# Second block: where the cycle without one two-head maximum stands in a hand-written order of attention work

## The chip, the cores and the metric

The kernel runs on one core of one Trainium2 chip. The metric is the device time of one execution in microseconds, the median of three runs. A profile is one further execution with the hardware profiler; its span is the time from the first to the last instruction on the engines.

## The reference, cut to what matters

Two independent attention blocks on 2048 tokens of width 512, with 32 heads of 16 each. Block A lets a query see the 256 keys up to itself, block B lets it see all keys. The outputs stand side by side.

```python
def _B_ref(x, wqkv, wo):
    B, S, D = x.shape
    H = 32
    Dh = D // H
    qkv = (lambda x, *d: x.transpose(*d))((x @ wqkv).reshape(B, S, 3, H, Dh), 2, 0, 3, 1, 4)
    q, k, v = qkv[0], qkv[1], qkv[2]
    scores = jnp.einsum("bhqd,bhkd->bhqk", q, k) * (Dh ** -0.5)
    p = _softmax(scores, axis=-1)
    o = jnp.einsum("bhqk,bhkd->bhqd", p, v)
    return (lambda x, *d: x.transpose(*d))(o, 0, 2, 1, 3).reshape(B, S, D) @ wo
```

`_A_ref` is the same with a mask: where a key lies after the query or 256 or more before it, the score is set to -1e9. The result is `concatenate([a, b], axis=-1)`, all in float32.

## The kernel before, in words

**Units and steps.** Work is cut into units (g, c): four heads (g of 8) by 512 queries (c of 4), so block B has 32 units. A unit takes 16 steps, one for each tile of 128 keys, 512 steps in all for block B, and `ns` counts four scores to a step. In a step TensorE multiplies keys by queries for four heads (`scores`, L572, one bank of PSUM each), ScalarE takes the exponential of each bank (L579), and TensorE, a step or two later, weighs the values with them (`weigh2`, L603). An extra row of ones in the values gives the sum for the softmax.

**The maxima.** The softmax needs the maximum of each row of scores before the exponential. So every score is also computed one unit ahead of its use, with queries on the partitions (`max2`, matmul L406), and VectorE reduces it (L410) into a tile `mt`. An item of this pass is 4 heads by 128 queries by 512 keys; a unit has 16 items, and there are 496 items from the second unit on (`mx`). An item consists of two halves of two heads each, counted by `half`. There are two ways to do a half:

- `M`: two matmuls into banks 3 and 4 and one VectorE reduction over both. The next `M` has to wait until this reduction has read the two banks.
- `m`, twice: one matmul into bank 5 or 6 and one reduction of one head each.

When both halves of an item are there, GpSimd (POOL) folds it into the running maximum (`chunk_max`: L514 for the first key chunk of four, otherwise L517, L518, L519). After the sixteenth item of a unit GpSimd splits the result into three bfloat16 parts (`low_finish`: L526 to L529, tile `nm`).

**The rows.** The maximum enters the scores as three extra rows of the queries' operand `oq`. `max_rows` makes them: TensorE transposes `nm` (L539, one load of weights and one matmul), ScalarE copies the result (L541), and two DMAs on SyncE's queue write it into `oq` (L546). The unit's scores wait for these DMAs. In the order below this is the letter `T`, and it does something once in a unit.

**The order.** All engines take their instructions in program order, so the order written for TensorE decides what waits for what. For block B it is written out as strings, worked through letter by letter: `s` one score, `M` and `m` as above, `2` and `4` a half or a whole step of weighing, `T` the rows, `x` one matmul of an output projection of block A or B, twelve to a tile of 128 tokens (L217).

- `ORDER` is the plain cycle of two steps: 8 `s`, 2 `M`, 4 `m`, so four halves. Its halves come in this sequence: a pair of `m`, `M`, a pair of `m`, and after `T` and one more `s` the second `M`.
- `ORDER_B` is `ORDER` without that second `M`: three halves in two steps.
- `ORDER_F` is the fed cycle of eight steps with a tile of twelve `x`: 32 `s`, 10 `M`, 12 `m`, so sixteen halves. It begins with `m s M`. It is chosen when a step divisible by 8 begins and a tile is due.
- `LAST` and `LAST_F` have no maxima and are used when all 496 items are done.

A tile is due (`due`, L1096) when its planned time has come and its operands are ready by the planner's own clock, or when one is begun. The step's number also releases loads and normalisations (`plan`, `settle`), and normalising puts three GpSimd operations into its queue (L690, L692, L693 of `normalise_now`).

**Which cycles occur.** Block B begins with step 2 of its loop; eleven plain cycles cover steps 2 to 23, sixteen fed cycles steps 24 to 151, 170 plain cycles steps 152 to 491, and cycles without maxima the rest. `ORDER_B` stands in the code of before, under the condition that a tile is due at the third plain cycle out of four; at the cycle of step 22 that isn't so yet, and behind it the fed cycles follow each other directly. So before has no `ORDER_B` cycle at all.

```python
ORDER = "ssm4mssMs2msms2TsM"
ORDER_B = "ssm4mssMs2msms2Ts"
ORDER_F = "msMs2mssm2ssMms4ssMms4ssMms4ssMsm4ssMms4mssMsxxxxxxTxxMsmss4MssmsxxxxsMsms4s"
```

Of the kernel before, what the change touches and what calls it, by code (L numbers as in the profile page):

```python
# [20 lines left out]
HG = 4  # L21
# [15 lines left out]
STEP = 2.36  # L37
# [3 lines left out]
# [3 lines that stand above are left out]
# [105 lines left out]
def attention_kernel(ctx: ExitStack, tc: tile.TileContext, xT, wqk, wv, wo, out):  # L149
# [9 lines left out]
    M = Model()  # L159
    ready = {}  # L160
    obank = [None]
    ns = 0
# [232 lines left out]
    def max2(g, c, qt, kc, heads, ps):  # L395

        m = maxima(1, g, c).rearrange("p (a r) q k -> p a r q k", a=2)
        early = g == 0 and c == 0 and heads[0] < 2
        if not early:
            follow(("k", 1, g))  # L400
            follow(("q", 1, g, c))
        for n, j in enumerate(heads):
            r, a = divmod(j, 2)
            rows = slice(ROW[a], ROW[a] + KS)
            q, k = (qe[0], ke()) if early else (opq[1, g, c][:, r], opk2(g)[:, r])
            nc.tensor.matmul(ps[:, n], q[rows, 128 * qt:128 * qt + 128], k[rows, kc * QC:kc * QC + QC], start=True,  # L406
                             stop=True)
            t = M.pe("h", 118, 0 if early else loaded(1, g, c))
        r, a = divmod(heads[0], 2)
        nc.vector.tensor_reduce(out=m[:, a:a + len(heads), r, qt, kc], in_=ps, axis=AX.X, op=ALU.max)  # L410
        return M.run("DVE", 65 + 533 * len(heads), t)
# [150 lines left out]
    def scores(b, g, c, kt, j, heads=1, pieces=((),)):  # L562

        n = f"{b}_{g}_{c}_{kt}"
        pr, a0 = divmod(j, 2)
        banks = [M.take("e") for _ in range(heads)]
        ps = [view(bank) for bank in banks]
        w = QC if b else sum(x[3] for x in pieces)
        for k, col, q0, n1 in [(kt, 0, 0, QC)] if b else pieces:
            for x in range(heads):  # L570
                rows = slice(ROW[a0 + x], ROW[a0 + x] + (KM if (b, g, c) > (1, 0, 0) else KS + 2))
                nc.tensor.matmul(ps[x][:, col:col + n1], opk2(g)[rows, pr, 128 * k:128 * k + 128],  # L572
                                 opq[b, g, c][rows, pr, q0:q0 + n1], start=True, stop=True)
            t = M.pe("h", 235 if b else 12 + n1 / 2.4, ready["q", b, g, c])
        if a0 == 0:
            pts[b, g, c, kt, pr] = sb.tile([128, 2, QC], F32, name=f"p_{n}_{pr}", tag="p", bufs=2 * AHEAD)
        p = pts[b, g, c, kt, pr]
        for x in range(heads):
            nc.scalar.activation(p[:, a0 + x, :w], ps[x][:, :w], AF.Exp, scale=SCALE)  # L579
            done = M.run("ACT", 60 + w / 1.2, t)  # L580
            M.release(banks[x], done)
        if b == 0:

            for d, sign, base in ((0, 1, 0), (2, -1, -1)):
                cols = [col // 128 + x for k, col, q0, n1 in pieces for x in range(n1 // 128)
                        if 4 * c + q0 // 128 + x - k == d]
                for x in cols:
                    v = p[:, :, 128 * x:128 * x + 128]
                    nc.gpsimd.affine_select(out=v, in_=v, pattern=[[0, 2], [sign, 128]], compare_op=ALU.is_ge,  # L589
                                            fill=zero_fill, base=base, channel_multiplier=-sign)  # L590
                    done = M.run("Pool", 360, done)
        ready["p", b, g, c, kt] = done
# [137 lines left out]
    proj = []  # L730
# [23 lines left out]
    def settle():  # L754

        while soon and soon[0][0] <= M.t["PE"]:
            heapq.heappop(soon)[2]()
# [34 lines left out]
    def pop():  # L792
        now[0], _, f, a = heapq.heappop(todo)
        f(*a)
        made.add((f, *a))

    gen = [None, None]
# [19 lines left out]
    def operands(it):  # L817

        f, b, *a = it
        if f == project_qk:  # L820
            keys = [(("w", b, a[0], a[1]), ("x", b, a[2], i)) for i in range(4)]
            t = slots_st[0] - 2700 + LAND_V
        elif f == project_v:
            keys = [(("w", b, "v", i), ("x", b, a[0], i)) for i in range(4)]
            t = slots_v[0] - 2700 + LAND_V
        else:
            keys = [(("w", b, "o", i), ("o", b, i, a[0])) for i in range(4 if len(a[1]) == 1 else 3)]
            t = 0
        at = [max(ready.get(x, M.NEVER) for x in k) for k in keys]
        return M.NEVER if max(at) >= M.NEVER else max(t, *(x - FEED * i * (f != project_out) for i, x in enumerate(at)))  # L830
# [115 lines left out]
    nm = k = nb = ne = n1 = 0  # L946
# [141 lines left out]
    mx = [(NA + 1 + i // 16, *units[NA + 1 + i // 16][1:], *divmod(i % 16, NQC)) for i in range(16 * turn)]  # L1088
    ns, nq, nm, fed = n1, n1 - 8, AHEADM, 0
    half, odd, full = 2 * AHEADM, None, set()  # L1090
    t0 = M.t["PE"] - 1000 * ns // HG * STEP
    rows, order = [], ORDER
    for u, g, c, qt, kc in mx[:AHEADM]:
        chunk_max(g, c, qt, kc)

    def due():  # L1096
        return gen[0] or proj and proj[0][0] <= ns // HG * STEP and operands(proj[0][3]) <= M.t["PE"]

    while nq < 4 * len(steps):
        if nm == len(mx) and len(M.banks["e"]) == 3:  # L1100
            M.banks["e"] += [M.t["PE"] + 4000] * 2
        if nm == len(mx):
            order = LAST_F if due() and not rows else LAST
        else:
            f, g = order == ORDER_F, ns // HG % 8
            order = ORDER_F if due() and g == 0 and nm + 8 <= len(mx) else ORDER
            if order == ORDER and not f and g == 6 and due() and nm + 10 <= len(mx):
                order = ORDER_B
        for x in order:
            k = ns // HG  # L1110
            if x == "s" and k < len(steps):
                if ns % HG == 0:
                    t = k * STEP
                    M.t["PE"] = max(M.t["PE"], t0 + int(1000 * k * STEP))
                    settle()
                    while todo and todo[0][0] <= t:
                        pop()
                scores(1, *steps[k], ns % HG)
                ns += 1
            elif x in "Mm" and (half < 2 * len(mx) or x == "m" and odd is not None):  # L1120
                if x == "M":
                    y = half
                    half += 1
                    max2(*mx[y // 2][1:], (2 * (y % 2), 2 * (y % 2) + 1), ps_all[:, 3:5])
                elif odd is None:
                    y, odd = half, half
                    half += 1
                    max2(*mx[y // 2][1:], (2 * (y % 2),), room()[1][:, None])
                else:
                    y, odd = odd, None  # L1130
                    max2(*mx[y // 2][1:], (2 * (y % 2) + 1,), room()[1][:, None])
                if y != odd:
                    full.add(y)
                while {2 * nm, 2 * nm + 1} <= full:
                    u, g, c, qt, kc = mx[nm]
                    chunk_max(g, c, qt, kc)
                    nm += 1
                    if nm % 16 == 0:
                        low_finish(g, c)
                        rows.append((k + 1, (1, g, c)))  # L1140
            elif x == "T":
                if rows and rows[0][0] + (nm == len(mx)) <= k:
                    max_rows(*rows.pop(0)[1])
            elif x == "x" and (gen[0] or due()):
                now[0] = k * STEP
                advance()
                fed += 1
                if fed == 12:
                    fed = 0
                    advance()  # L1150
                    if nm < len(mx):
                        t0 += 2410
            elif x.isdigit():
                if 0 <= nq < 4 * len(steps):
                    g, c, kt = steps[nq // 4]
                    q = nq % 4
                    weigh2(g, c, kt, 128 * q, 128 * (q + int(x)))
                    if kt == NT - 1 and q + int(x) == 4:
                        unit_end(1, g, c)
                nq += int(x)  # L1160
# [29 lines left out]
```

## Time and profile before

| what | value |
|---|---|
| time, median of 3 runs | 1818.95 us (1818.33 to 1819.58) |
| the profiled execution's own time | 1819.65 us |
| span of the profiled execution | 1817.9 us |
| ScalarE busy in the span | 1420.0 us (78%) |
| GpSimd busy in the span | 688.8 us (38%) |
| VectorE: L410, the maxima of block B | 1203.4 us, 1482 reductions |
| TensorE: L572, L406, L603 | 739.4, 636.3, 586.8 us |

The rows of a view of instructions read: start and length in microseconds, engine, line, operation, tiles and shapes, count of merged instructions, and in brackets the idle time of the engine before it with what ended it. PE is TensorE's matmuls, PEld its loads of weights. A row that merges several instructions of an engine runs from the start of the first to the end of the last. A view of windows gives for each stretch its bounds, its length, then each engine's busy time with the number of instructions, the granted clock of TensorE and the DMA share. Reductions on VectorE are pipelined, so one starts up to 0.1 us before the end of the one before.

### The profile page before, as it was taken

The numbers are of one execution on the slowest core, as the hardware profiler recorded it, in microseconds if no ns is written. First come the engines' busy times: TensorE is split into PE (matmuls) and PEld (weight loads), VectorE is DVE, ScalarE is ACT, GpSimd is POOL, SyncE is SP. The second block draws the span as 40 slices with busy tenths as digits, with TensorE's granted clock in tenths as the row PEclk, the third lists the DMA queues.
The fourth block names the chain that finished last, engine by engine and source line by source line (L and its number), as shares of the span: only waits on it lengthen the run. The fifth ranks groups of instructions, "written<-read, shape, count | busy, mean of one in ns | idle before, by whom it ended". The sixth has DMA issues, their size and how long they took to land. (4 is left out here: it accounts for less than half of the span.)

```text
span 1817.9 us, 38163 instructions
## 1 busy us (share of the span) xinstructions
PE 1798.2 (99%) x13992; PEld 901.4 (50%) x13992; DVE 1515.2 (83%) x2189; ACT 1420.0 (78%) x2773; POOL 688.8 (38%) x2054
## 2 busy tenths in 40 slices
PE   7999999999999999999999999999999999999999
PEld 5766666666664444444444444444444444444446
DVE  4655676766689889999989999999999999999911
ACT  4367777565659788888889988998898998899883
POOL 0167787554655453223222423332222333222310
PEclk9999999999999999999999999999999999999999
DMA  7756767454553225111300311030030121000012
GB/s 239 198 177 200 225 206 220 152 164 140 180 182 104 71 74 117 45 42 40 75 28 26 74 47 39 29 78 17 16 76 29 35 63 37 17 24 15 30 34 97
DMA packets 128569, 166.47 MB, mean 92 GB/s; under 512 B 22946, under 2 KB 58258, under 8 KB 128370
## 3 DMA queue, kind: packets, MB, share of 16 engines
q1 hardware_dynamic: 128382, 164.04, 31.2%
q8 instruction: 110, 1.80, 0.4%
q14 instruction: 77, 0.63, 0.1%
HBM read 94.49 MB, written 68.19 MB: 89 GB/s over the span
## 5 line engine op out<-in xcount | busy, mean ns | idle before, releaser
L579 ACT ACTIVATE p<-ps_all 128x512 f32<-128x512 f32 x2432 | 1257.8, 598 | 163.1 <-PE ps_all L572 116.0
L410 DVE TENSOR_REDUCE mt<-ps_all 128x1 f32<-128x512 f32 (+1 forms) x1482 | 1203.4, 884 | 53.3 <-PE ps_all L406 38.2
L572 PE MATMUL ps_all<-oq,opk 51*128 51x512 f32 (+3 forms) x2752 | 739.4, 406 | 2.4 <-ACT p L579 2.1
L406 PE MATMUL ps_all<-opk,oq 48*128 48x512 f32 x2016 | 636.3, 433 | 1.0 <-DVE mt L410 1.0
L603 PE MATMUL ps_all<-p,vt 128*32 128x256 f32 (+1 forms) x5672 | 586.8, 487 | 0.0
L572 PEld LDWEIGHTS ps_all<-oq,opk 51*128 51x128 f32 (+1 forms) x2752 | 376.8, 185 | 227.7 <-ACT p L579 196.0
L406 PEld LDWEIGHTS ps_all<-opk,oq 48*128 48x128 f32 x2016 | 303.1, 185 | 277.7 <-issue 149.7
L517 POOL TENSOR_TENSOR md<-mt,mm 128x4 f32<-128x4 f32 x372 | 75.9, 204 | 612.2 <-DVE mt L410 611.2
L589 POOL TENSOR_SCALAR_AFFINE_SELECT p<-p 128x256 f32<-128x256 f32 x480 | 178.9, 406 | 221.9 <-ACT p L579 220.4
L603 PEld LDWEIGHTS ps_all<-p,vt 128*32 128x32 f32 x5672 | 112.7, 108 | 218.1 <-issue 208.1
L217 PE MATMUL ps_all<-x,w 128*128 128x512 f32 x768 | 195.1, 404 | 10.3 <-ACT w L170 10.2
L463 DVE COPY_PREDICATED ps_all<-mone,ps_all 128x256 f32<-128x256 uint16 x224 | 95.0, 424 | 85.8 <-PE ps_all L454 84.1
L217 PEld LDWEIGHTS ps_all<-x,w 128*128 128x128 f32 x768 | 141.2, 190 | 50.5 <-ACT w L170 10.2
L464 DVE TENSOR_REDUCE mt<-ps_all 128x2 f32<-128x512 f32 x224 | 155.2, 693 | 7.7
L279 ACT ACTIVATE raw<-ps_all 128x512 f32<-128x512 f32 x56 | 33.5, 598 | 108.8 <-PE ps_all L217 105.9
L217 PE MATMUL ps_all<-w_o,x_o 128*128 128x512 f32 x384 | 102.3, 407 | 0.2 <-ACT ob L715 0.2
L217 PE MATMUL ps_all<-w_v,x 128*128 128x512 f32 x384 | 96.4, 400 | 0.3 <-DVE w_v L171 0.3
L618 PE MATMUL ps_all<-p,vt 128*32 128x384 f32 (+2 forms) x1408 | 96.4, 390 | 0.0
L518 POOL TENSOR_SCALAR md<-md 128x4 f32<-128x4 f32 x372 | 81.7, 220 | 32.6
L454 PE MATMUL ps_all<-opk,oq 48*128 48x384 f32 (+2 forms) x512 | 88.1, 373 | 1.3 <-DVE mt L464 1.1
L519 POOL TENSOR_TENSOR mm<-mm,md 128x4 f32<-128x4 f32 x372 | 74.8, 201 | 31.0
L217 PEld LDWEIGHTS ps_all<-w_o,x_o 128*128 128x128 f32 x384 | 68.0, 188 | 26.9 <-issue 8.0
(63 smaller groups left out, 718.3 us busy)
## 6 DMA issues: line engine op xcount, KB each, us to landing
parts<-st SPq DMA_DIRECT2D x64, 512.0 KB
opk<-parts SPq DMA_DIRECT2D x128, 128.0 KB
oq<-parts SPq DMA_DIRECT2D x128, 128.0 KB
od<-ou SPq DMA_DIRECT2D x64, 256.0 KB
vd<-vst SPq DMA_DIRECT2D x32, 272.0 KB
opk<-parts SPq DMA_DIRECT2D x128, 64.0 KB
oq<-parts SPq DMA_DIRECT2D x128, 64.0 KB
t<-od SPq DMA_DIRECT2D x32, 256.0 KB
```

The source lines that it names most:

```text
L217: nc.tensor.matmul(ps, l(u), r(v), start=start and k == 0, stop=stop and k == n - 1)
L406: nc.tensor.matmul(ps[:, n], q[rows, 128 * qt:128 * qt + 128], k[rows, kc * QC:kc * QC + QC], start=True, stop=True)
L410: nc.vector.tensor_reduce(out=m[:, a:a + len(heads), r, qt, kc], in_=ps, axis=AX.X, op=ALU.max)
L454: nc.tensor.matmul(two[:, a, 0:w], opq[b, g, c][rows, r, 128 * qt:128 * qt + 128], opk2(g)[rows, r, t0:t1], start=True, stop=True)
L463: nc.vector.copy_predicated(two[:, :, 256:384], later, two[:, :, 0:128])
L464: nc.vector.tensor_reduce(out=m[:, :, r, qt, 0], in_=two[:, :, 128:384], axis=AX.X, op=ALU.max)
L518: nc.gpsimd.tensor_scalar(d, d, 0.0, None, op0=ALU.max)
L572: nc.tensor.matmul(ps[x][:, col:col + n1], opk2(g)[rows, pr, 128 * k:128 * k + 128], opq[b, g, c][rows, pr, q0:q0 + n1], start=True, stop= ...
L579: nc.scalar.activation(p[:, a0 + x, :w], ps[x][:, :w], AF.Exp, scale=SCALE)
L589: nc.gpsimd.affine_select(out=v, in_=v, pattern=[[0, 2], [sign, 128]], compare_op=ALU.is_ge, fill=zero_fill, base=base, channel_multiplier ...
L603: nc.tensor.matmul(o[32 * j:32 * j + 32, q0:q1], vt[(g // 2) % 2][:, kt, vc:vc + 32], pts[1, g, c, kt, j // 2][:, j % 2, q0:q1], start=kt ...
L618: nc.tensor.matmul(o[32 * j:32 * j + 32, q0:q0 + w], vt[(g // 2) % 2][:, kt, vc:vc + 32], pts[b, g, c, m, j // 2][:, j % 2, col:col + w], ...
```

## The change

`due` can look ahead by a number of steps, with a twentieth more: a tile counts as due if its planned time and its operands' time lie no more than 2.1 steps (4.96 us of the planner's clock) ahead. The cycle of a step with remainder 6 by 8 becomes `ORDER_B` the first time that a tile is due two steps ahead, and never again (`shorter`). The conditions on a preceding fed cycle and on ten items left are dropped.

```diff
@@ -1089,12 +1089,13 @@
     ns, nq, nm, fed = n1, n1 - 8, AHEADM, 0
     half, odd, full = 2 * AHEADM, None, set()
     t0 = M.t["PE"] - 1000 * ns // HG * STEP
-    rows, order = [], ORDER
+    rows, shorter = [], True
     for u, g, c, qt, kc in mx[:AHEADM]:
         chunk_max(g, c, qt, kc)
 
-    def due():
-        return gen[0] or proj and proj[0][0] <= ns // HG * STEP and operands(proj[0][3]) <= M.t["PE"]
+    def due(ahead=0):
+        d = (ahead + ahead / 20) * STEP
+        return gen[0] or proj and proj[0][0] <= ns // HG * STEP + d and operands(proj[0][3]) <= M.t["PE"] + 1000 * d
 
     while nq < 4 * len(steps):
         if nm == len(mx) and len(M.banks["e"]) == 3:
@@ -1102,10 +1103,10 @@
         if nm == len(mx):
             order = LAST_F if due() and not rows else LAST
         else:
-            f, g = order == ORDER_F, ns // HG % 8
+            g = ns // HG % 8
             order = ORDER_F if due() and g == 0 and nm + 8 <= len(mx) else ORDER
-            if order == ORDER and not f and g == 6 and due() and nm + 10 <= len(mx):
-                order = ORDER_B
+            if shorter and g == 6 and due(2):
+                order, shorter = ORDER_B, False
         for x in order:
             k = ns // HG
             if x == "s" and k < len(steps):
```

**At the entry of the first fed cycle.** TensorE's rows around step 24, where the plain cycle of step 22 ends and the first fed cycle begins; L406 is a matmul of the maxima, L572 a score, L603 weighing. Before:

```order
L572 MATMUL ps_all<-oq_0_1_5847,opk_74 128x512
L406 MATMUL ps_all<-opk_74,oq_0_2_6059 128x512 x3
L572 MATMUL ps_all<-oq_0_1_5847,opk_74 128x512
L406 MATMUL ps_all<-opk_74,oq_0_2_6059 128x512 x2
L572 MATMUL ps_all<-oq_0_1_5847,opk_74 128x512
L603 MATMUL ps_all<-p_0_1_6_0_7034,vt_76 32x256 x2
```

The same rows of TensorE at the same place after the change:

```order
L572 MATMUL ps_all<-oq_0_1_5847,opk_74 128x512
L406 MATMUL ps_all<-opk_74,oq_0_2_6059 128x512
L572 MATMUL ps_all<-oq_0_1_5847,opk_74 128x512
L406 MATMUL ps_all<-opk_74,oq_0_2_6059 128x512 x2
L572 MATMUL ps_all<-oq_0_1_5847,opk_74 128x512
L603 MATMUL ps_all<-p_0_1_6_0_7034,vt_76 32x256 x2
```

Of the three maxima matmuls in the second row, two are the plain cycle's second `M`; they are gone, and the fed cycle's first `m` is left. The two matmuls of the fourth row are the fed cycle's first `M`.

**From there on.** The number of halves to be done is the same, so every place in the order now holds the half that stood one place later before, until the maxima end. Sixteen halves fill a fed cycle and four a plain one, so nothing evens this out. TensorE's rows in the plain cycle that holds the `T` of unit (7, 0), long after the fed cycles; `oq_7_0` names the unit whose maxima are being taken, `oq_7_1` the next one, `oq_6_3` the unit whose scores run. Before:

```order
L406 MATMUL ps_all<-opk_75,oq_7_0_18189 128x512 x2
L572 MATMUL ps_all<-oq_6_3_17739,opk_74 128x512 x2
L406 MATMUL ps_all<-opk_75,oq_7_1_18631 128x512
L603 MATMUL ps_all<-p_6_3_10_0_19014,vt_77 32x512 x2
L603 MATMUL ps_all<-p_6_3_10_1_19027,vt_77 32x512 x2
L406 MATMUL ps_all<-opk_75,oq_7_1_18631 128x512
...
L539 LDWEIGHTS nm_7_0_19067
L539 MATMUL ps_all<-ident,nm_7_0_19067 48x128
```

And TensorE's rows at the same place after the change:

```order
L406 MATMUL ps_all<-opk_75,oq_7_0_18176 128x512 x2
L572 MATMUL ps_all<-oq_6_3_17726,opk_74 128x512 x2
L406 MATMUL ps_all<-opk_75,oq_7_0_18176 128x512
L603 MATMUL ps_all<-p_6_3_10_0_19007,vt_77 32x512 x2
L603 MATMUL ps_all<-p_6_3_10_1_19024,vt_77 32x512 x2
L406 MATMUL ps_all<-opk_75,oq_7_0_18176 128x512
...
L539 LDWEIGHTS nm_7_0_19082
L539 MATMUL ps_all<-ident,nm_7_0_19082 48x128
```

The last half of unit (7, 0) was the second `M` of the cycle before; it is now the first pair of `m` of the cycle that holds the transposition, which itself has not moved.

At the end of the maxima one half is left over: steps 492 and 493 form a plain cycle with two `m` in place of two `LAST` cycles, the last `T` moves from the end of step 493 to the end of step 494, and the `LAST_F` cycles begin at step 495 in place of 494.

**On GpSimd.** A normalisation's three operations (L690, L692, L693) stay where the step's number puts them in GpSimd's queue, while the last item of a unit moves back past them. GpSimd's rows around the end of the maxima of unit (1, 0), in a fed cycle; `md_0_3_2` and `md_0_3_3` are the fifteenth and the sixteenth item, `t_3_3` is block A's normalisation of the last chunk, and L526 begins the splitting. Before:

```order
L517 TENSOR_TENSOR md_0_3_2_8138<-mt_1_0_7689,mm_0_7711 128x4
L518 TENSOR_SCALAR md_0_3_2_8138<-md_0_3_2_8138 128x4
L519 TENSOR_TENSOR mm_0_7711<-mm_0_7711,md_0_3_2_8138 128x4
L517 TENSOR_TENSOR md_0_3_3_8157<-mt_1_0_7689,mm_0_7711 128x4
L518 TENSOR_SCALAR md_0_3_3_8157<-md_0_3_3_8157 128x4
L519 TENSOR_TENSOR mm_0_7711<-mm_0_7711,md_0_3_3_8157 128x4
L526 CAST nm_1_0_8161<-mm_0_7711 128x2x8
L527 TENSOR_TENSOR nr_1_0_8162<-mm_0_7711,nm_1_0_8161 128x16
L528 CAST nm_1_0_8161<-nr_1_0_8162 128x2x8
L529 TENSOR_TENSOR nm_1_0_8161<-nr_1_0_8162,nm_1_0_8161 128x2x8
L690 TENSOR_TENSOR t_3_3_8110<-t_3_3_8110,bl_3_3_8112 128x512
L692 CAST x_o_3_3_8182<-t_3_3_8110 128x512
```

GpSimd's rows at the same place after the change:

```order
L517 TENSOR_TENSOR md_0_3_2_8135<-mt_1_0_7692,mm_0_7752 128x4
L518 TENSOR_SCALAR md_0_3_2_8135<-md_0_3_2_8135 128x4
L519 TENSOR_TENSOR mm_0_7752<-mm_0_7752,md_0_3_2_8135 128x4
L690 TENSOR_TENSOR t_3_3_8103<-t_3_3_8103,bl_3_3_8105 128x512
L692 CAST x_o_3_3_8168<-t_3_3_8103 128x512
L693 TENSOR_TENSOR x_o_3_3_8168<-t_3_3_8103,x_o_3_3_8168 128x512
L517 TENSOR_TENSOR md_0_3_3_8182<-mt_1_0_7692,mm_0_7752 128x4
L518 TENSOR_SCALAR md_0_3_3_8182<-md_0_3_3_8182 128x4
L519 TENSOR_TENSOR mm_0_7752<-mm_0_7752,md_0_3_3_8182 128x4
L526 CAST nm_1_0_8186<-mm_0_7752 128x2x8
L527 TENSOR_TENSOR nr_1_0_8187<-mm_0_7752,nm_1_0_8186 128x16
L528 CAST nm_1_0_8186<-nr_1_0_8187 128x2x8
```

The normalisation of `t_3_3` stood behind the splitting and now stands between the fifteenth and the sixteenth item.

## The prediction

> **What bounds the kernel now.** I read the page first, then windows, then single rows. The page gives the span and TensorE's share:
>
> ```profile
> span 1817.9 us, 38163 instructions
> PE 1798.2 (99%) x13992; PEld 901.4 (50%) x13992; DVE 1515.2 (83%) x2189; ACT 1420.0 (78%) x2773; POOL 688.8 (38%) x2054
> ```
>
> A PE that is 99% busy is no proof of a bound, since matmuls overlap. So I cut block B into stretches: fed cycles of eight steps, the whole plain stretch, and the steps behind the maxima. Each row gives the length, then the busy time of each engine, and the granted clock ahead of the DMA share.
>
> ```profile
> core 0: us, PE busy (x) PEld busy (x) DVE busy (x) ACT busy (x) POOL busy (x), PEclk, DMA share, GB/s
> 592.81:618.67 25.86, 24.86 (x151) 9.80 (x150) 20.40 (x24) 17.46 (x34) 12.64 (x32) 0.87 0.12 36
> 618.67:639.66 20.99, 20.99 (x150) 9.18 (x148) 19.13 (x23) 17.61 (x34) 10.93 (x25) 1.00 0.32 102
> 639.66:661.63 21.97, 21.49 (x151) 9.18 (x150) 19.12 (x23) 17.43 (x35) 13.71 (x36) 1.00 0.33 79
> 661.63:682.65 21.02, 21.02 (x150) 9.11 (x149) 19.16 (x23) 17.61 (x34) 10.91 (x25) 1.00 0.23 77
> 682.65:704.06 21.41, 21.41 (x151) 9.18 (x150) 19.13 (x23) 17.43 (x34) 12.22 (x34) 1.00 0.32 81
> 595.90:602.72 6.82, 6.82 (x36) 2.25 (x36) 3.95 (x6) 3.87 (x8) 4.60 (x11) 0.50 0.10 35
> 937.00:1731.00 794.00, 794.00 (x6819) 333.78 (x6819) 792.93 (x1028) 715.22 (x1402) 230.69 (x966) 1.00 0.15 38
> ```
>
> Two things stand out. In the plain stretch VectorE is busy 792.93 of 794.00 us: it is the bound there, with 1.07 us to spare. In fed cycles it is not (19.13 of 20.99 us); TensorE is, with twelve more matmuls. And the first fed cycle takes 25.86 us where the third and the fifth, which like the first hold a transposition, take 21.97 and 21.41: something is lost at its entry, the place that the change is about.
>
> **The entry, which gets faster.** TensorE's and VectorE's rows there:
>
> ```profile
> 592.03 0.94 PE L406 MATMUL ps_all<-opk,oq 48*128 48x512 f32 x3
> 592.81 0.40 PE L572 MATMUL ps_all<-oq,opk 51*128 51x512 f32 x1
> 594.21 0.50 PE L406 MATMUL ps_all<-opk,oq 48*128 48x512 f32 x2 [1.00 <-DVE mt L410]
> 592.34 1.81 DVE L410 TENSOR_REDUCE mt<-ps_all 128x1 f32<-128x512 f32 x2
> ```
>
> The x3 holds the plain cycle's last `M`; VectorE reduces it last in the row that ends at 594.15. The fed cycle's own `M` needs the same two banks, and TensorE stands still for 1.00 us. Soon after, the window from 595.90 shows a granted clock of 0.50 for 6.82 us, which costs about half of that, 3.41 us. Together 4.41 us, and the windows say 25.86 - 21.41 = 4.45: the two agree. With the change the `M` in front is gone, its banks were read a half cycle earlier, and the wait has no cause. What is late next is VectorE, still one one-head reduction behind at the entry; against that the cycle in front has one reduction less. I take **-4.5 us**, with ends of -3 (a shorter wait stays) and -5.5 (the cycle in front is shorter by all its reduction). The reduction is not saved, only done later.
>
> The Trainium skill, "TensorE: Matmul & The Clock Gate", section "HAM oscillation", gives as its rule that no idle gap of TensorE over about 3.4 us should occur. Here 1.00 us of idle time stands ahead of the half clock, so the trace does not agree. By that rule the clock would not hang on this wait, and the term would be about -1.0 us.
>
> **The transpositions, which get slower.** The rest of the program runs one half later. In the plain stretch the cycle that holds `T` is this:
>
> ```profile
> 1621.07 1.27 DVE L410 TENSOR_REDUCE mt<-ps_all 128x1 f32<-128x512 f32 x2
> 1623.99 1.85 DVE L410 TENSOR_REDUCE mt<-ps_all 128x1 f32<-128x512 f32 x2
> 1621.29 0.21 POOL L517 TENSOR_TENSOR md<-mt,mm 128x4 f32<-128x4 f32 x1 [1.53 <-DVE mt L410]
> 1622.99 0.22 POOL L529 TENSOR_TENSOR nm<-nr,nm 128x16 bf16<-128x16 f32 x1
> 1623.67 0.10 PEld L539 LDWEIGHTS <-nm 128*48 128x48 bf16 x1 [0.41 <-POOL nm L529]
> 1624.18 0.40 PE L406 MATMUL ps_all<-opk,oq 48*128 48x512 f32 x1
> ```
>
> Before, the unit's last half is an `M` that ends as the pair of the first row begins. GpSimd folds and splits from 1621.29 to 1623.21, and TensorE comes to L539 at 1623.67, 0.46 us later: covered. After, the last half is the pair of the first row. Its end is 1622.34, two one-head reductions later. Their spacing is 1.27 us less the length of one:
>
> ```profile
> L410 DVE TENSOR_REDUCE mt<-ps_all x1018: 622/680/1227, 936.9 to 1729.9; 128x2 f32<-128x1024 f32 x169, 128x1 f32<-128x512 f32 x1
> ```
>
> So 1.27 - 0.68 = 0.59 us each and 1.19 for two. GpSimd's chain then ends at 1623.21 + 1.19 = 1624.40, L539 starts at 1624.45 (0.05 after it, as at 654.58 below), and TensorE waits 0.78 us longer. Behind the waiting L539 stand a score and the second `M`. In before that `M` is ready at 1624.18 + 0.40 = 1624.58, and VectorE is through with the pair of the second row at about 1624.6: nothing is in stock. So VectorE idles as long as TensorE does, and since it is the bound of this stretch the loss stays. ScalarE waits for the score too, but has 794.00 - 715.22 us of slack. The rows' copy and two DMAs move with L539, and so do the scores that need them. With 0.03 us taken off I count 0.75 us for each. How many there are:
>
> ```profile
> L539 PE MATMUL ps_all<-ident,nm x21: 236/237/237, 950.7 to 1698.5; 128*48 128x128 bf16 x21
> L539 PE MATMUL ps_all<-ident,nm x7: 236/237/237, 654.6 to 909.2; 128*48 128x128 bf16 x7
> ```
>
> In the plain stretch 21, so **+15.8 us**; ends are 0 (if VectorE makes it up) and 21 x 0.78 = 16.4. Seven, with one more in the first fed cycle, lie in fed cycles. One of them:
>
> ```profile
> 735.32 0.20 POOL L517 TENSOR_TENSOR md<-mt,mm 128x4 f32<-128x4 f32 x1 [0.51 <-DVE mt L410]
> 737.01 0.22 POOL L529 TENSOR_TENSOR nm<-nr,nm 128x16 bf16<-128x16 f32 x1
> 737.77 0.23 POOL L514 TENSOR_SCALAR mm<-mt 128x4 f32<-128x4 f32 x1 [0.54 <-DVE mt L410]
> 739.44 0.24 PE L539 MATMUL ps_all<-ident,nm 128*48 128x128 bf16 x1
> ```
>
> L514 belongs to the next half's item, so 737.77 is when the last fold can begin after the change. From 735.32 to 737.23 the chain takes 1.91 us, so it ends at 739.68, and L539 starts at 739.73: 0.29 us late. That such a wait is paid in full shows in the unit whose GpSimd is late already:
>
> ```profile
> 654.31 0.22 POOL L529 TENSOR_TENSOR nm<-nr,nm 128x16 bf16<-128x16 f32 x1
> 654.58 0.24 PE L539 MATMUL ps_all<-ident,nm 128*48 128x128 bf16 x1 [0.48 <-POOL nm L529]
> ```
>
> Its fed cycle took 21.97 us against 21.41: 0.56 us for 0.48 of idle matmul time. There the chain is held up by something else and I add nothing. Six units at 0.3 make **+1.8 us**, with ends 0 and 2.4.
>
> The eighth is unit (1, 0), where a normalisation now stands ahead of the last item:
>
> ```profile
> 691.00 1.29 POOL L693 TENSOR_TENSOR x_o<-t,x_o 128x512 fp32r<-128x512 f32 x1
> 692.24 0.23 POOL L517 TENSOR_TENSOR md<-mt,mm 128x4 f32<-128x4 f32 x1
> 693.13 0.20 POOL L517 TENSOR_TENSOR md<-mt,mm 128x4 f32<-128x4 f32 x1
> 688.96 1.28 POOL L690 TENSOR_TENSOR t<-t,bl 128x512 f32<-128x512 f32 x1 [0.35 <-DMA bl<-rl]
> 697.02 0.24 PE L539 MATMUL ps_all<-ident,nm 128*48 128x128 bf16 x1
> ```
>
> Three such operations take 692.29 - 688.96 = 3.33 us, one item 0.89. After the item at 692.24 come 3.33 us and the 1.91 of the chain: 693.13 + 3.33 + 1.91 + 0.05 = 698.42, so L539 is **1.4 us** late; 0 if the operations are done sooner, 3.3 if their DMA lands late.
>
> **The end.** Behind the maxima the last `T` comes one step later:
>
> ```profile
> 1734.39 0.73 PE L572 MATMUL ps_all<-oq,opk 51*128 51x512 f32 x3
> 1736.99 0.24 PE L539 MATMUL ps_all<-ident,nm 128*48 128x128 bf16 x1
> 1740.80 0.73 PE L572 MATMUL ps_all<-oq,opk 51*128 51x512 f32 x4
> ```
>
> A `LAST` step takes 1736.99 - 1734.39 = 2.6 us. After the change two steps run as a plain cycle, at the stretch's pace of (1698.5 - 950.7) / 20 / 16 = 2.34 a step, and one remains. From T to the unit's first score there are then 3.81 us in place of two steps more, for the copy and two DMAs. I count **0**, with ends of -1 and +1.
>
> **The sum.** -4.5 + 15.8 + 1.8 + 1.4 + 0 = +14.5 us on the profiled execution's 1819.65 us, whose span of 1817.9 is 1.75 shorter. That is 1834.1. The median of the runs is 0.7 us lower, so I predict **1833.4 us**.
>
> **The rivals.** *The waits at `T` are absorbed.* GpSimd's chain may be released earlier than I take it, or TensorE may come to `T` later, once VectorE is behind it. Then only the entry's gain is left: 1819.0 - 4.5 = 1814.5. It speaks for it that 0.46 us of cover exist, against it that the reductions' order and the distance to `T` can be read off; it decides where the delay falls below 0.46 us, and it is 1.19. I give it 0.11. *Half of it is absorbed*, for instance because TensorE's faster stretches refill VectorE: +8 - 4.5 + 1.6, so 1824; 0.10. Near zero, 1816 to 1822, lies 0.06.
>
> *The new waits bring down the clock.* TensorE would be idle about as long before `T` as the 1.00 us at the entry. If each of 21 brought 6.82 us at 0.50, that is 21 x 3.41 = 72 us more: 1905. Against it, the wait of 0.48 us at 654.58 has 1.00 around it, and after `T` the matmuls go on densely, which at the entry they did not. I give 0.06 to many, and 0.15 of the main case to one or two, 3.4 us each. The Trainium skill, same page, section "A second HAM failure mode: psum-queue depth-cycling", tells of small idle times between groups of matmuls that let the clock swing to and fro. That speaks for this rival; no run here shows it so far.
>
> **How the numbers follow.** The forecast, 1827 to 1840, has 0.67, the absorbed half 0.10, absorbed 0.11, near zero 0.06, clock 0.06. The range 1822 to 1841 holds the first two, 0.77 and part of the near ones. A measurement can tell 0.2% (3.6 us) from no change. Faster 0.11, same 0.07, slower 0.82.
>
> **What would show it.** The first fed cycle near 21.4 us at clock 1.00; idle time before L539 of about 1.2 us, put down to L529, in each of the 21 plain units; units of 38.1 us in place of 37.4; VectorE near 98% in the plain stretch; one late L539 in unit (1, 0). Wrong would be: L539 released without a longer wait, VectorE still at 99.9%, or clock windows of 0.50 after `T`.

## The result, and the profile after

The changed kernel takes 1839.41 us (median of 4 runs, 1836.60 to 1841.02) against 1819.05 us (4 runs on the same chip, 1818.33 to 1819.58): slower by a factor of 1.0111, with a 95% interval of 1.0093 to 1.0128. The profiled execution took 1836.60 us.

The same lines of the page as before, and of its groups L410 (VectorE's reductions of the maxima) and L603 (TensorE's weighing); behind the last bar stand the idle time in front of the group and what ended most of it:

```profile
span 1834.9 us, 38157 instructions
PE 1796.6 (98%) x14000; PEld 897.7 (49%) x14000; DVE 1515.9 (83%) x2190; ACT 1425.1 (78%) x2773; POOL 692.1 (38%) x2054
L410 DVE TENSOR_REDUCE mt<-ps_all 128x1 f32<-128x512 f32 (+1 forms) x1483 | 1204.1, 887 | 69.4 <-PE ps_all L406 44.8
L603 PE MATMUL ps_all<-p,vt 128*32 128x256 f32 (+1 forms) x5680 | 585.9, 485 | 1.4 <-ACT ou L629 1.4
```

The row of L410 before:

```profile
L410 DVE TENSOR_REDUCE mt<-ps_all 128x1 f32<-128x512 f32 (+1 forms) x1482 | 1203.4, 884 | 53.3 <-PE ps_all L406 38.2
```

TensorE's and VectorE's busy times hardly moved; the span grew by 17.0 us, and the idle time in front of VectorE's reductions by 16.1 us. So it is idle time, and the windows say where: the first fed cycle, that of unit (1, 0), and the plain stretch.

```profile
core 0: us, PE busy (x) PEld busy (x) DVE busy (x) ACT busy (x) POOL busy (x), PEclk, DMA share, GB/s
592.07:613.81 21.74, 21.45 (x151) 9.10 (x148) 19.11 (x23) 17.36 (x34) 13.08 (x30) 1.00 0.14 43
677.80:700.84 23.04, 21.49 (x153) 9.21 (x150) 19.14 (x23) 17.43 (x34) 11.86 (x31) 1.00 0.29 76
937.00:1731.00 794.00, 778.73 (x6687) 324.36 (x6679) 777.83 (x1008) 705.78 (x1375) 228.83 (x953) 1.00 0.14 37
```

The first fed cycle is short and at full clock (25.86 us and 0.87 before). Unit (1, 0) takes 23.04 us for 21.41. In the plain stretch VectorE, busy 792.93 us of 794.00 before, is now busy 777.83. A plain cycle with `T`, in rows of the timeline of VectorE, GpSimd, TensorE's loads and TensorE:

```profile
1632.36 4.74 DVE L410 TENSOR_REDUCE mt<-ps_all 128x2 f32<-128x1024 f32 x6
1637.84 1.82 DVE L410 TENSOR_REDUCE mt<-ps_all 128x2 f32<-128x1024 f32 x2 [0.74 <-PE ps_all L572]
1634.92 0.21 POOL L517 TENSOR_TENSOR md<-mt,mm 128x4 f32<-128x4 f32 x1 [1.53 <-DVE mt L410]
1636.63 0.22 POOL L529 TENSOR_TENSOR nm<-nr,nm 128x16 bf16<-128x16 f32 x1
1636.90 0.10 PEld L539 LDWEIGHTS <-nm 128*48 128x48 bf16 x1 [1.21 <-POOL nm L529]
1636.90 0.24 PE L539 MATMUL ps_all<-ident,nm 128*48 128x128 bf16 x1 [0.72 <-POOL nm L529]
1637.07 0.73 PE L406 MATMUL ps_all<-opk,oq 48*128 48x512 f32 x2
```

Read it from the bottom. The matmuls of the next maximum (L406) stand behind `T`; `T` (L539) starts 0.05 us after GpSimd's L529 ends; L529 is the last of a chain that L517 began when VectorE had given the unit's last reduction. TensorE's matmuls stood still for 0.72 us, and VectorE then had nothing to reduce for 0.74 us. The load of weights waited 1.21 us; before it was 0.41, and no matmul waited. All 21 units of the stretch do so. The answer for line L539 between 930 and 1715 gives, after the instructions, the idle time of loads and matmuls together (42 is twice 21):

```profile
L539 PE MATMUL ps_all<-ident,nm x21: 236/237/237, 950.2 to 1713.2; 128*48 128x128 bf16 x21
  POOL nm L529: 40.7, 42
```

It gives the measure used below too: from one `T` to the next (1713.2 - 950.2) / 20 = 38.15 us, where before it was (1698.5 - 950.7) / 20 = 37.39.

### The profile page after: what moved, and what is told of

It is laid out like the page before. It is cut to its first block, busy times and chain, and to the rows that moved or that the text cites. A ratio compares the mean times of both kernels' runs of the same rounds, so it can differ in the third digit from the quotient of the medians.

```text
span 1834.9 us, 38157 instructions
## 1 busy us (share of the span) xinstructions
PE 1796.6 (98%) x14000; PEld 897.7 (49%) x14000; DVE 1515.9 (83%) x2190; ACT 1425.1 (78%) x2773; POOL 692.1 (38%) x2054
## 5 line engine op out<-in xcount | busy, mean ns | idle before, releaser
L410 DVE TENSOR_REDUCE mt<-ps_all 128x1 f32<-128x512 f32 (+1 forms) x1483 | 1204.1, 887 | 69.4 <-PE ps_all L406 44.8
L572 PE MATMUL ps_all<-oq,opk 51*128 51x512 f32 (+3 forms) x2752 | 740.6, 405 | 1.9 <-ACT p L579 1.7
L406 PE MATMUL ps_all<-opk,oq 48*128 48x512 f32 x2016 | 631.8, 432 | 0.0
L603 PE MATMUL ps_all<-p,vt 128*32 128x256 f32 (+1 forms) x5680 | 585.9, 485 | 1.4 <-ACT ou L629 1.4
L572 PEld LDWEIGHTS ps_all<-oq,opk 51*128 51x128 f32 (+1 forms) x2752 | 376.0, 185 | 227.2 <-ACT p L579 194.7
L406 PEld LDWEIGHTS ps_all<-opk,oq 48*128 48x128 f32 x2016 | 299.5, 184 | 276.1 <-DVE mt L410 159.9
L517 POOL TENSOR_TENSOR md<-mt,mm 128x4 f32<-128x4 f32 x372 | 76.6, 206 | 577.0 <-DVE mt L410 574.4
L603 PEld LDWEIGHTS ps_all<-p,vt 128*32 128x32 f32 x5680 | 112.5, 108 | 219.9 <-issue 208.0
L514 POOL TENSOR_SCALAR mm<-mt 128x4 f32<-128x4 f32 x124 | 28.7, 232 | 169.9 <-DVE mt L410 169.9
```

What stands on the lines that cost most here:

```text
L603: nc.tensor.matmul(o[32 * j:32 * j + 32, q0:q1], vt[(g // 2) % 2][:, kt, vc:vc + 32], pts[1, g, c, kt, j // 2][:, j % 2, q0:q1], start=kt ...
```

## The experiments

Times are medians beside the kernel before on the same chip (1820.21 us for the first four runs, 1819.87 for the next four, 1819.81 for the last four). A unit is the distance between two `T` in the plain stretch; VectorE is its busy time in the 778.00 us from 937 to 1715.

| run | us (lowest to highest) | ratio to before, 95% | unit, us | VectorE, us |
|---|---|---|---|---|
| before | 1819.05 | | 37.39 | 776.93 |
| the change | 1839.41 (1836.60 to 1841.02) | 1.0093 to 1.0128 | 38.15 | 761.83 |
| e1_again | 1837.29 (1836.69 to 1838.10) | 1.0078 to 1.0108 | 38.14 | 761.89 |
| e2_made_up | 1817.10 (1816.41 to 1818.63) | 0.9975 to 0.9994 | 37.39 | 777.89 |
| e3_T_later | 1831.14 (1830.55 to 1832.47) | 1.0045 to 1.0075 | 37.86 | 768.20 |
| e4_T_earlier_before | 1837.28 (1835.85 to 1839.49) | 1.0080 to 1.0114 | 38.19 | 763.49 |
| e5_T_next_cycle | 1834.68 (1833.49 to 1836.21) | 1.0068 to 1.0096 | 37.99 | 765.51 |
| e6_T_next_both | 1832.34 (1831.70 to 1832.81) | 1.0052 to 1.0083 | 37.99 | 765.66 |
| e7_pair_before | 1818.96 (1816.24 to 1821.74) | 0.9987 to 1.0005 | 37.40 | 777.88 |
| e8_end_before | 1821.55 (1820.23 to 1822.31) | 0.9999 to 1.0016 | 37.39 | 776.89 |
| e9_longer_chain_before | 1843.67 (1842.77 to 1848.23) | 1.0122 to 1.0149 | 38.41 | 756.78 |
| e10_shorter_chain_after | 1817.75 (1816.75 to 1819.98) | 0.9980 to 0.9998 | 37.37 | 778.00 |
| e11_shorter_chain_made_up | 1816.62 (1815.05 to 1817.28) | 0.9973 to 0.9991 | 37.40 | 777.84 |
| e12_shorter_chain_T_next | 1830.82 (1829.50 to 1833.49) | 1.0046 to 1.0077 | 37.99 | 766.40 |

### The change once more

The changed kernel, unaltered.

> The changed kernel once more, for its spread. Its four runs so far lie between 1836.6 and 1841.0 us, with granted clocks of 1.000, 0.998, 0.999 and 0.998. If the new waits ahead of the transpositions sometimes bring a stretch of half clock, runs again fall apart by steps of some 2 to 3.5 us and the mean clock goes down with the time; a profile then shows a stretch of 0.50 behind one of the waits. If the spread is something else, time and clock do not go together.

It came out 2.1 us lower than the first time. All four of its runs had a mean clock of 1.000, of the first four only the fastest had; the others had 0.998 or 0.999. So the change costs about 17 us, and the rest of the first result goes with a lower mean clock.

### The late half given back

The changed kernel, with one more `M` in the first fed cycle after the short cycle:

```diff
+ORDER_F1 = "msMs2mssm2ssMms4ssMms4ssMms4ssMsm4ssMms4mssMsxxxxxxTxxMsmss4MssmsxxMxxsMsms4s"
             order = ORDER_F if due() and g == 0 and nm + 8 <= len(mx) else ORDER
+            if order == ORDER_F and half % 2:
+                order = ORDER_F1
```

> The change, with the missing half made up by one more M in the first fed cycle, so that every later place holds the half that it held before. Theory (the loss is the lag of one half at the transposition T): the 21 plain waits and all fed ones but the first go, the entry keeps its gain of 4.1 us, the end is as before: 1819 - 4.1 + 0.4 = 1815.3 us, up to 1816 if the additional M waits. Rival (the loss comes from the short cycle or the entry themselves, not from the lag): about 1839 us.

The unit is back at 37.39 us, VectorE at 777.89 of 778.00. So nothing after the first fed cycle is slow but for the lag. The first fed cycle takes 23.30 us, with the extra half in it, against 25.86 before and 21.74 in the change; the extra half thus costs 1.6 us, more than was expected, and the time lies 1.1 us above the expectation's upper end. The kernel is faster than both: than before by 3.1 us, with an interval that ends at 0.9994.

### The transposition in another place

The plain cycle with its `T` two letters later, on the changed kernel; and, on the kernel before, where nothing lags, some letters earlier:

```diff
-ORDER = "ssm4mssMs2msms2TsM"
+ORDER = "ssm4mssMs2msms2sMT"
```

> The change, with T moved behind the second M of the plain cycle, some 0.8 us later; the lag of one half stays. Theory: the 21 waits of 0.78 us for GpSimd are covered, VectorE has its M ahead of T and does not idle, 15.9 us go; the fed cycles keep their 3.7 us and the entry its gain: 1819 - 4.1 + 3.7 = 1818.7 us, with VectorE at 99.8% in the plain stretch. Rival (the lag starves VectorE in another way): 1833 us or more.

```diff
-ORDER = "ssm4mssMs2msms2TsM"
+ORDER = "ssm4mssMs2mTsms2sM"
```

> The kernel before, with T moved four letters earlier in the plain cycle, about 1.07 us; no half is moved. Theory (a TensorE that waits at T takes VectorE's stock away): TensorE waits 1.07 - 0.46 = 0.6 us in each of 21 plain units, VectorE idles about 0.55: 1819 + 21 x 0.55 = 1830.5 us. Rival (the stock carries VectorE over such a wait, and the loss needs the lag): 1819 to 1821 us.

Both missed, in the same direction: dearer than the wait alone. e4 shows that `T` ahead of its data costs as much as the change without any lag; but its load of weights waited only 0.22 us longer than before (0.63 for 0.41), and its unit grew by 0.80 us. In e3 the load waited 0.08 us longer than before, and yet only 0.29 of the 0.76 us a unit were won back. Then still later, behind two scores of the next cycle, in the plain cycle alone and in both:

```diff
-ORDER = "ssm4mssMs2msms2TsM"
+ORDER = "ssTm4mssMs2msms2sM"
```

> The changed kernel with only the plain cycle's T moved on, behind the first two scores of the cycle that follows (ssTm4mssMs2msms2sM), some 0.5 us of TensorE's own work later than in the run e3_T_later, where the plain cycles with a T still took 5.26 us against 4.83 before. Theory (what costs is TensorE standing still before T until GpSimd's last L529 ends, which starves VectorE): the chain has ended by then, the 21 plain T cycles fall from 5.61 to about 4.83, 16.4 us together, and the time goes from 1837.3-1839.4 to 1821-1823; VectorE is idle about 1 us in the 778 us from 937 to 1715 instead of 16.2. Rival A (the lag of one half costs by itself, or T does where a four-wide weighing follows): the cycles stay at 5.2 as in e3_T_later, 1830-1831. Rival B (the row now lands too late for the next unit's first score, some 4 us behind): new waits at L572 at each unit's start, 1831 or more.

And with that, for e6:

```diff
-ORDER_F = "msMs2mssm2ssMms4ssMms4ssMms4ssMsm4ssMms4mssMsxxxxxxTxxMsmss4MssmsxxxxsMsms4s"
+ORDER_F = "msMs2mssm2ssMms4ssMms4ssMms4ssMsm4ssMms4mssMsxxxxxxxxMsmssT4MssmsxxxxsMsms4s"
```

> As e5_T_next_cycle, and in the fed cycle too T stands later, behind the half of two single heads' worth of scores that followed it (xxxxxxxxMsmssT4M instead of xxxxxxTxxMsmss4M). Theory: the six fed cycles with a T fall from 6.22 to 5.79 us, 2.6 us together, so 1818.5-1820.5, what is left over before being the unit (1,0) (+1.6) and the end (+1.4 and +1.1) less the entry (-4.1). Rival: the fed cycles with the feeds moved together take longer for the burst of two more x, 0.3 us each, and nothing is won against e5_T_next_cycle: 1821-1823.

Rival A of e5: the unit stays at 37.99, and the time lies even above that rival's range. Rival B is out: TensorE stands idle before no score of the plain stretch. In e6 the unit stays there too, so e6 missed both its theory and its rival. Its later `T` in the fed cycles brings little: the six whose `T` waited on account of the lag are 0.11 to 0.20 us shorter than in the change, where 0.43 was expected. Unit (1, 0) takes 22.19 us in the profiled execution of e6 and 25.32 in that of e5, where `T` waited 2.31 us and the half clock followed. So a place is good or bad beyond whether the data is there, and these four runs cannot size the wait. That took the chain itself.

### The chain longer, the chain shorter

On the kernel before, GpSimd's L527 six times:

```diff
-        nc.gpsimd.tensor_sub(r1, mr, nm[0])
+        for _ in range(6):
+            nc.gpsimd.tensor_sub(r1, mr, nm[0])
```

> The kernel before with GpSimd's chain made longer and nothing else: the subtraction of L527 is issued six times instead of once, five more instructions some 0.285 us apart, so 1.43 us more. In the profile of before the chain of a plain T ended 0.46 us ahead of it (L529 to 1623.21, T at 1623.67); it would now end 0.97 us late, as late as in the changed kernel. No half lags behind and T stands where it stood. Theory (the wait of T for this chain is the whole price, at 0.8 us a wait of 0.97): the 21 plain T cycles go from 4.83 to about 5.6 and the fed ones from 5.79 to about 6.2, so +15 to +19 us, 1835-1839. Rival (the lag of one half costs by itself, by the order in which TensorE and VectorE meet, and the wait only goes along): under +8, 1820-1828.

On the changed kernel, a chain without L527 to L529:

```diff
-        nc.gpsimd.tensor_sub(r1, mr, nm[0])
-        nc.gpsimd.tensor_copy(nm[1], r1)
-        nc.gpsimd.tensor_sub(nm[2], r1, nm[1])
...
+                    if nm % 16 == 14:
+                        nm_tiles(1, g, c)
+                        nc.gpsimd.memset(parts["nm"][:, :, 1:3], 0.0)
```

> The changed kernel with GpSimd's chain made shorter and nothing else: of the three bf16 parts of the negated maximum only the first is formed (L526); the other two are set to zero two chunks ahead, so the subtraction, the copy and the second subtraction (L527 to L529) leave the chain and it ends 0.84 us sooner. (It leaves out the low parts of the maximum, which shift all scores of a query alike.) The lag stays. Theory: the wait of a plain T falls from 0.97 to about 0.13 us, its cycle from 5.61 to 4.85-4.95; with the fed ones 14 to 18 us less than the changed kernel: 1820-1825. Rival (the lag by itself): 1834-1839, no change.

They decide it. The timeline's load at one `T` of e10:

```profile
1657.16 0.10 PEld L534 LDWEIGHTS <-nm 128*48 128x48 bf16 x1 [0.41 <-POOL nm L524]
```

With the lag kept and the chain short, the unit takes 37.37 us, the load at `T` waits 0.41 us as before, and all of the loss in the plain stretch is gone. The fed cycles that waited for the lag are back as well, at 21.38 to 21.57 us, and the time lies 2.3 us below the expectation. With no lag and a long chain, `T` waits as in the change, only longer; the timeline of e9:

```profile
1602.87 0.20 POOL L517 TENSOR_TENSOR md<-mt,mm 128x4 f32<-128x4 f32 x1 [1.53 <-DVE mt L410]
1604.01 1.68 POOL L528 TENSOR_TENSOR nr<-mm,nm 128x16 f32<-128x16 f32 x6
1606.03 0.22 POOL L530 TENSOR_TENSOR nm<-nr,nm 128x16 bf16<-128x16 f32 x1
1606.30 0.10 PEld L540 LDWEIGHTS <-nm 128*48 128x48 bf16 x1 [1.45 <-POOL nm L530]
1607.24 1.23 DVE L410 TENSOR_REDUCE mt<-ps_all 128x2 f32<-128x1024 f32 x1 [0.99 <-PE ps_all L573]
```

(Line numbers are one higher.) Taken from the load's 0.41 us before, the wait grew by 0.80 us in the change and by 1.04 here; the unit by 0.76 and 1.02. In this place a wait is paid in full. The result of e9 lies 4.7 us above its expectation, which took 0.97 for the wait of the changed kernel, the mean of the load's and the matmul's; it is the load's that compares, and 21 times 0.24 is 5 us. In seven of the eight fed cycles with a `T` the two steps with it stayed at 5.77 to 5.81 us, and not at the 6.2 expected, since 2.2 us of cover lie there (737.23 to 739.44 before) and the chain grew by 1.46.

The same short chain on the two other orders:

> e2_made_up (no lag, the late half given back in the first fed cycle) with the shorter chain of e10_shorter_chain_after (the same low parts left out). Theory: no T waits there, so a shorter chain finds nothing to win: 1816.5-1817.5. Rival (a T cycle takes 4.83 against 4.62 of a cycle without T because of the chain): up to 21 times 0.2 less, 1813.

> e5_T_next_cycle with the shorter chain of e10_shorter_chain_after (the same low parts left out). There T stood behind the first two scores of the next cycle, waited only about 0.2 us for GpSimd and 0.2 for ScalarE to free a bank, and its cycle took 5.46 all the same. Theory A (what is left is still the wait for the chain): 4.85, 1834.7 less 13, 1821-1823. Theory B (that place is bad by itself: T asks for a score bank and sits ahead of a four-wide weighing, and VectorE runs dry behind it): the cycle stays at 5.3 to 5.46, 1831-1835.

e11 is the fastest kernel of all, but its interval overlaps that of e2: where no `T` waits, a shorter chain brings nothing that can be told. Theory B holds for e12: no wait for the chain is left, and the unit still takes 37.99 us. What its `T` waited for, and VectorE behind it:

```profile
  issue: 5.2, 21
  ACT p L574: 4.5, 21
1669.21 0.22 PE L534 MATMUL ps_all<-ident,nm 128*48 128x128 bf16 x1 [0.21 <-ACT p L574]
1671.31 1.83 DVE L410 TENSOR_REDUCE mt<-ps_all 128x1 f32<-128x512 f32 x2 [0.54 <-PE ps_all L567]
```

There `T` asks for a bank that ScalarE has not freed (0.21 us), and a four-wide weighing of 1.07 us comes before the second of the next maxima; VectorE runs dry for 0.54 us. This is read from the rows: no run takes the weighing or the bank away. e5, which differs only in the chain, has the same unit. For e3 and e4 such a reason was only argued.

### The entry

The kernel before, with the half in front of the first fed cycle as two single heads in place of `M`:

```diff
+ORDER_C = "ssm4mssMs2msms2Tsmm"
-            if order == ORDER and not f and g == 6 and due() and nm + 10 <= len(mx):
-                order = ORDER_B
+            if ns // HG == 22:
+                order = ORDER_C
```

> The kernel before with only the last half in front of the first fed cycle written as two single-head maxima (mm) in place of the two-head maximum M: no half is left out, nothing lags behind, so no T waits. Theory (the loss of 4.1 us in the first fed cycle comes from a two-bank maximum that stands right in front of it: TensorE waits for VectorE to free both banks, and the half clock follows): the entry becomes as short as in the changed kernel, T stays as before, 1815.5-1816.5 against 1820.2. Rival (VectorE's queue is full with that half whichever way it is written, so TensorE waits for it all the same and the half clock comes as before): 1819.5-1820.5.

Neither theory: five of its runs took 1816.24 to 1817.41 us, all at clock 1.000, and six 1818.96 to 1821.74, all at 0.998. The profiled one is among the first; its windows of the cycle of step 22 and of the first fed cycle:

```profile
587.37:593.70 6.33, 6.05 (x45) 2.46 (x43) 6.33 (x10) 4.82 (x10) 5.35 (x11) 1.00 0.55 129
593.70:615.08 21.38, 21.38 (x150) 9.11 (x148) 19.10 (x23) 17.00 (x33) 11.50 (x31) 1.00 0.12 38
```

The cycle of step 22 takes 6.33 us, against 5.05 before, and VectorE is busy in all of it. So the two banks are not the cause: VectorE is behind by that half, and TensorE waits for it in either form: the cycle is 1.28 us longer here, and 1.00 us of idle time stood at the entry before. With `M` most runs have a mean clock below 1 (19 of the 21 beside it had 0.998 or 0.999), with two `m` about half. Between e7's two groups lie some 3.7 us. In the changed kernel VectorE does one half less there, where it has no time to spare. It does not catch up in the fed cycles, though it has time in them (19.11 us busy of 21.74): each holds as many halves as before, and the one left over is done behind step 491, when VectorE has little else to do.

### The end

The kernel before, with `LAST_F` allowed only from step 495 on, as it falls in the changed kernel:

```diff
-            order = LAST_F if due() and not rows else LAST
+            order = LAST_F if due() and not rows and ns // HG > 494 else LAST
```

> The kernel before with only the closing order begun one step later (from step 495, as the changed kernel does, instead of 494). Theory (the changed kernel's step 496 lost 1.4 us because the unit boundary now falls on the second of two four-wide weighings in a row, and the new unit's weighing waits for ScalarE to copy the output bank behind eight exponentials): +1.4 us, and up to +1.1 at the tail, 1821.4-1822.7 against 1820.2. Rival (the loss at the end belongs to the late T, not to where the closing order begins): 1820.2, no change.

The theory's mechanism is in its trace, ScalarE's row first:

```profile
1743.28 4.25 ACT L579 ACTIVATE p<-ps_all 128x512 f32<-128x512 f32 x8 [0.51 <-PE ps_all L572]
1747.39 0.63 ACT L629 ACTIVATE ou<-ps_all 128x512 f32<-128x512 f32 x1
1748.07 1.06 PE L603 MATMUL ps_all<-p,vt 128*32 128x512 f32 x8 [1.41 <-ACT ou L629]
```

TensorE waits 1.41 us, as in the changed kernel's own rows:

```profile
1758.15 4.27 ACT L579 ACTIVATE p<-ps_all 128x512 f32<-128x512 f32 x8 [0.51 <-PE ps_all L572]
1762.29 0.63 ACT L629 ACTIVATE ou<-ps_all 128x512 f32<-128x512 f32 x1
1762.97 1.06 PE L603 MATMUL ps_all<-p,vt 128*32 128x512 f32 x8 [1.41 <-ACT ou L629]
```

Two steps of weighing stand in a row in `LAST_F` ("44"). The unit's end now falls between them, so the new unit's weighing needs the output bank that ScalarE must first copy (`ou`), behind eight exponentials. The time rose by 1.7 us, though the interval, 0.9999 to 1.0016, just includes none. The other traces bear the mechanism out. In the profiles of all seven runs in which `LAST_F` begins one step later (e8, the change, e1, e5, e6, e10, e12) TensorE waits 1.41 us there, in the other seven it does not. One of those is e3, which has the lag but begins `LAST_F` where before does.

## Why the prediction came out as it did

The steps, in the profiled executions (from the starts of the scores, L572; the end is everything from step 488 on; what lies ahead of step 24 is scatter, since block B's first score starts between 534.0 and 536.0 us in the fourteen profiles):

| step | predicted | measured |
|---|---|---|
| entry | -4.5 | -4.5 |
| 21 plain `T` | +15.8 | +15.9 |
| fed `T` | +1.8 | +2.4 |
| unit (1, 0) | +1.4 | +1.6 |
| the end | 0 | +2.2 |
| ahead of step 24 | none | -0.7 |
| sum | +14.5 | +17.0 |

**The entry** has the right size: steps 24 to 27 went from 14.43 to 9.93 us, full clock included. Its reason was half right. The wait and the half clock are as described, but e7 shows that the `M`'s two banks are not what binds; VectorE's backlog is, which the prediction named only as what is late next. And 3.4 of the 4.5 us hang on the half clock, which by their mean clock most runs of before have, but not all.

**The plain transpositions.** "TensorE waits 0.78 us longer" and "idle time before L539 of about 1.2 us": 0.80 and 1.21. "VectorE idles as long as TensorE does", and since it is the bound the loss stays: shown from both sides by e9 and e10. The two rivals in which the wait is absorbed fall with that.

**The fed transpositions.** 0.3 us each was too small: the two steps with `T` went from 5.80 to 6.23, in the first fed cycle from 5.79 to 6.16. The step took the fold's start from the next half's item, L514 at 737.77, which was 0.1 us early. The same unit after:

```profile
734.55 0.20 POOL L517 TENSOR_TENSOR md<-mt,mm 128x4 f32<-128x4 f32 x1 [3.08 <-DVE mt L410]
736.26 0.22 POOL L529 TENSOR_TENSOR nm<-nr,nm 128x16 bf16<-128x16 f32 x1
736.53 0.10 PEld L539 LDWEIGHTS <-nm 128*48 128x48 bf16 x1 [0.77 <-POOL nm L529]
736.53 0.24 PE L539 MATMUL ps_all<-ident,nm 128*48 128x128 bf16 x1 [0.34 <-POOL nm L529]
```

The load waited 0.36 us before, so 0.41 more.

**Unit (1, 0).** The normalisation stands in GpSimd's queue as expected, and TensorE waits for what comes after it:

```profile
688.48 1.28 POOL L690 TENSOR_TENSOR t<-t,bl 128x512 f32<-128x512 f32 x1
690.52 1.29 POOL L693 TENSOR_TENSOR x_o<-t,x_o 128x512 fp32r<-128x512 f32 x1
691.77 0.21 POOL L517 TENSOR_TENSOR md<-mt,mm 128x4 f32<-128x4 f32 x1
693.75 0.24 PE L539 MATMUL ps_all<-ident,nm 128*48 128x128 bf16 x1 [1.55 <-POOL nm L529]
```

**The end** is the step that failed, by 2.2 us. It looked only for the row's landing, and there nothing waits. Missed was that `LAST_F` begins at another step, so that the unit's end meets the double weighing: 1.4 us, shown by the traces named under e8. Another 1.0 us lies behind the start of the last step's scores; e8 has it too (39.94 us from there to the end, 38.96 before, 39.95 after). In the seven profiles with the later `LAST_F`, 24 weighing matmuls are left behind that point, in the others 16.

**The rest** of the distance, from 1833.4 to 1839.41, is 2.5 us of the sum and 3.5 us between the profiled execution and the median, which was taken to lie 0.7 us below it and lies 2.8 above. The profiled execution had a mean clock of 1.000, the other three had less. That fits the prediction's "one or two" stretches of 3.4 us each, but where they lay in those runs wasn't profiled. One place is known from e10 and e12, which carry the lag too: step 494 has the half clock in their profiles and takes 5.89 and 5.88 us, against 4.38 in the change's. The rival with a half clock at many waits is out: 1.00 in the whole plain stretch, with 21 waits in it.

## What to carry to other kernels

Where a hand-written order has a fixed number of places, taking one item out shifts every later item by one; follow the shifted item to the tightest dependence that it meets once a period, and multiply. If the order must be opened in one place, give the item back at the next stage with slack, as e2 does. And a chain of small operations between two engines that are both full is worth shortening before anything is moved around it: e10 kept the lag and lost nothing, though its chain is shorter only because it leaves out the low parts of the maximum.

## What the runs showed of the hardware

The half clock followed single waits of TensorE that were not long. In e9 the `T` at 653.17 had 1.94 us of idle time ahead of it; a window before and one after it:

```profile
652.00:653.00 1.00, 0.00 (x0) 0.00 (x0) 0.00 (x0) 0.00 (x0) 0.72 (x4) 1.00 0.00 0
656.00:658.00 2.00, 2.00 (x10) 0.83 (x6) 1.01 (x2) 0.57 (x2) 0.63 (x3) 0.50 0.02 5
```

In e5 it came behind a `T` that waited 2.31 us. The changed kernel's 1.55 us in unit (1, 0) and its 21 waits of 0.72 us brought none in its profiled execution, while 1.00 us did at the entry of before. In step 494 of e10 it came behind a wait of 0.22 us; the change has the same wait, 0.21 us, at the same place, and kept the full clock. Windows at the wait and after it, two of e10 and then two of the change:

```profile
1733.00:1734.00 1.00, 0.78 (x3) 0.36 (x2) 0.00 (x0) 1.00 (x3) 0.86 (x3) 1.00 0.00 0
1735.00:1737.00 2.00, 2.00 (x11) 0.66 (x4) 0.00 (x0) 0.45 (x2) 0.26 (x1) 0.50 0.00 0
1751.00:1752.00 1.00, 0.79 (x4) 0.34 (x2) 0.00 (x0) 0.88 (x3) 0.92 (x3) 1.00 0.00 0
1753.00:1755.00 2.00, 2.00 (x13) 0.77 (x5) 0.00 (x0) 1.02 (x3) 1.63 (x2) 1.00 0.00 0
```

So neither the length of one wait nor its place in the program settles it; how dense the matmuls around it are may, which no run here isolates. The Trainium skill, "TensorE: Matmul & The Clock Gate", section "HAM oscillation", sets the limit for an idle gap at about 3.4 us; the gaps of 0.22, 1.00, 1.94 and 2.31 us here are shorter, and the measurement decides.

Apart from that, a transposition of 0.24 us, its data ready, costs 0.2 or 0.8 us by its place among the same letters: the two steps with it take 4.84 us before and 5.46 in e12, the cycles without it 4.65 on average in both.
